# Attention in front of a two-layer network: the maxima of queries and keys behind the third sigmoid's split, their product with ones in the next pair, and ten output steps in a batch's first gap

## The chip, the core and the metric

The kernel runs on one core of a Trainium2 chip. The core has four engines that compute: TensorE (matmuls into PSUM; PE in the profile, its weight loads PEld), VectorE (DVE), ScalarE (ACT) and GpSimd (POOL). SyncE (SP) issues the transfers. Each engine works through its own list of instructions in order, and engines wait for each other through semaphores. The metric is the device time of one execution in microseconds, the median of several.

## The reference

```python
def _attn_ref(q, k, v) -> np.ndarray:          # (8, 12, 448, 64) each
    S = q.shape[2]
    scale = 1.0 / np.sqrt(q.shape[-1])
    scores = scale * np.matmul(q, k.transpose(0, 1, 3, 2)) - np.log(S)
    attn = 1.0 / (1.0 + np.exp(-scores))
    return np.matmul(attn, v).astype(np.float32)

def _moe_ref(x, w_in, w_out) -> np.ndarray:    # (3584, 768), (768, 2048), (2048, 768)
    h = x @ w_in
    alpha = 1.0
    g = np.where(h > 0.0, h, alpha * (np.exp(np.minimum(h, 0.0)) - 1.0))
    return (g @ w_out).astype(np.float32)
```

The attention's result, its heads side by side, is the network's x. So each of the 8 batches has 12 heads of 448 tokens, a sigmoid in place of a softmax, and 448 rows of the network.

## The kernel before

**Numbers as pairs of halves.** A float32 operand is split into a high and a low float16 part (`split`, L120: ScalarE writes the high part, VectorE the low one), and a product takes three matmuls: high x high, low x high, high x low. Before a split the operand is multiplied by a power of two that comes from its largest magnitude. `prepare` (L294) finds the maxima of a pair of heads per partition on VectorE (L125 for values, mx, and for queries and keys, mt; L307, L310), and puts them on the diagonal of a matrix (`magnitude`, L98: three instructions of L105 write dg). That is its first part. The second part, `scales` (L314), multiplies ones with that matrix on TensorE (L110, pb: the "product with ones", which brings all 128 partitions' maxima to each), takes the largest (L112), rounds it to a power of two (L113, L114), and makes the scales on VectorE and GpSimd (L318, L324, L319, L322, L289; the tile sc). The third part, `transposed` (L331), splits queries and keys by those scales (nat, three pieces on each of the two engines), has a DMA transpose them into qk (L352), and splits the values (vn, L358).

**A pair of heads.** The loop from L686 on runs over batches 1 to 7 and, in each, over six pairs. For a pair, `scores` (L376) multiplies keys by queries for one of four blocks of keys (t = 0 to 3, the last of them half as large) into psc, of which there are two buffers. `soften` (L391) takes the sigmoid on ScalarE (sg, L395), and for the first three blocks splits it: high part on ScalarE (at, L413), low part on VectorE (at, L414). `values` (L419) multiplies values by those into pav; each block's last two matmuls are the first that read the low part. `finish` splits the result into xh, the network's input (L121, L122), and takes its maximum.

**The network.** Behind the sixth pair, `hidden` rescales xh (L448, L450, L451), and `moe1` (L479) multiplies it by w_in for 16 blocks of the hidden layer (ph), with the exponential on ScalarE. Behind ph's first block stands a product with ones of its own, for the layer's scale. The output layer of a batch (`moe2`) is not run then: it is cut into steps of three matmuls (po, L529; 16 steps to a tile, 96 steps, or 128 where two batches' last tokens are done too) that the next batch's pairs run between their own work. `fill(n)` runs n such steps. Batches 1, 3, 5 and 7 have 96 steps, 16 for a pair; batches 2, 4 and 6 have 128, 21 or 22 for a pair. Those of the first kind are called short below.

**What sets the order.** Batch 0, the weights' splits and the first layer of batch 0 are put in order by a planner from a model of times. From L685 on, the order on TensorE, ScalarE, VectorE and SyncE is that of the code; GpSimd's is planned. In the loop, a pair n does: scores and sigmoids of blocks 0 and 1; `third()`, the split and transpose of pair n+1; the loads of pair n+3; a gap of 8 steps in a batch's first pair and 5 in the others; the maxima of pair n+2 (`prepare_pair`); scores and sigmoids of blocks 2 and 3; the rest of the steps; the product and scales of pair n+2 (`second()`); the values; `finish`. In batch 1 the last splits of w_out (`step`, wo) are in the loop too.

Of the kernel before, what the change touches and what calls it, by code (L numbers as in the profile page):

```python
# [32 lines left out]
def attention_ffn(  # L33
# [13 lines left out]
    NP = H // 2  # L47
# [9 lines left out]
    EXACT = 1  # L57
# [213 lines left out]
    def load_v(b, hp):  # L271
        rv = rvs[(b * NP + hp) % len(rvs)]
        main = rv[:, : 2 * NC].rearrange("p t d -> p (t d)")
        load_keys(main, [rv[r, 2 * NC + j] for j, r in enumerate(rows)], v, b, 2 * hp)
        return rv
# [320 lines left out]
    def prepare_pair(n):  # L596

        if n >= len(pairs):
            return lambda: lambda: None
        b, hp = pairs[n]  # L600
        if hp == 0:
            xh_of[b] = sb.tile([P, NK, 2, S], F16, tag="xh", name=f"xh{b}", bufs=2)
            xs_of[b] = sb.tile([P, 3, NP], F32, tag="xs", name=f"xs{b}", bufs=2)
        scales = prepare(b, hp, *loaded.pop(n), xs_of[b])

        def second():
            transposed = scales()

            def third():
                ready[n] = transposed()  # L610

            return third

        return second
# [12 lines left out]
    def pair_of(n):  # L627
        b, hp = pairs[n]
        return Pair(b, hp, *ready.pop(n), xh_of[b], xs_of[b])
# [18 lines left out]
    def load_pair(n):  # L648
        if n < len(pairs):
            loaded[n] = load_qk(*pairs[n]), load_v(*pairs[n])  # L650
# [8 lines left out]
    for n in range(EXACT * NP):  # L659
# [12 lines left out]
        for f in range(W_IN[n], W_IN[n + 1]):  # L672
            load_w_in(1)
            w_in_tile(f)
    third = prepare_pair(EXACT * NP + 1)()
    load_pair(EXACT * NP + 2)
    g = sb.tile([P, 2, NF, SM + 2 * R], F16, tag="g", name="g")
    h = hidden(0, w_out_beside)
# [6 lines left out]
    with tc.manual_schedule(engines={E.PE, E.Activation, E.DVE, E.SP}):  # L685
        for b in range(EXACT, B):  # L686
            out_scale(*of_moe2, slice(0, 1 if b == EXACT else NH))
            tiles = moe2(b - 1, g, wo)
            left = NF * NH * (NC + (b - 1) % 2)

            def fill(n):
                nonlocal left
                left -= n
                for _ in range(n):
                    next(tiles, None)

            for hp in range(NP):
                n = b * NP + hp
                share = left // (NP - hp)
                tail = 4 if hp == NP - 1 else 0  # L700
                p = pair_of(n)
                for t in range(2):
                    p.scores(t)
                    p.soften(t)
                third()
                if n + 3 < len(pairs):
                    loaded[n + 3] = load_qk(*pairs[n + 3]), load_v(*pairs[n + 3])

                gap = 8 if hp == 0 else 5
                fill(gap)  # L710
                second = prepare_pair(n + 2)
                for t in range(2, NC + 1):
                    p.scores(t)
                    p.soften(t)
                if b == EXACT and hp < NC:

                    step(3 if hp < NC - 1 else NF)
                if hp == NP - 1:
                    h = hidden(b)
                    next(h)  # L720
                fill(share - gap - tail)
                third = second()
                for t in range(NC + 1):
                    p.values(t)
                p.finish()
                fill(tail)
                if b == EXACT and hp == NC - 1:
                    out_scale(*of_moe2, slice(1, NH))
            of_moe2 = next(h)
        out_scale(*of_moe2)  # L730
        for _ in moe2(B - 1, g, wo):
            pass
# [30 lines left out]
```

## Time and profile before

| | |
|---|---|
| runs of the kernel before | 1273.72, 1271.79, 1272.22 us; median 1272.22 |
| the profiled execution | 1270.86 us, its span 1269.1 us |
| busy, share of the span | TensorE 95%, VectorE 65%, ScalarE 53%, GpSimd 7% |
| HBM over the span | 55 GB/s |
| mean granted TensorE clock | 0.984 |

A row of the timeline reads: start in us from the span's start, duration, engine, line, operation, output and inputs by name, shape, and how many instructions are merged. In brackets stands how long the engine had been idle and what released it. A row of the waits reads: who waited, for whom, us in total, how often, the longest. A row of the stretches reads: the stretch, its length, the busy time of PE, PEld, DVE, ACT and POOL with instructions in brackets, the granted clock, the DMA's share and GB/s.

### The profile page before, as it was taken

The page shows a single profiled execution, that of the slowest core. Times are in us where ns is not written, and L with a number is a line of the kernel's source. Part 1 is how long each engine was busy: PE and PEld are TensorE (multiplying, and loading weights), DVE is VectorE, ACT ScalarE, POOL GpSimd, SP SyncE. Part 2 cuts the span into 40 slices and gives each one's busy share as a digit, 9 for nine tenths or more (in the row PEclk, how much of TensorE's full clock was granted, in tenths as well). Part 3 has the DMA queues.
Part 4 walks back from the last instruction along what each step waited for, and adds up shares of the span by engine and source line. Part 5 has one row for each costly group of instructions (what it writes and reads, how often), then busy time and mean ns, then how long its engine had stood idle before and what let it go on. Part 6 is the DMA issues. An engine that isn't in the chain of part 4 may idle for free.

```text
span 1269.1 us, 19337 instructions
## 1 busy us (share of the span) xinstructions
PE 1200.2 (95%) x7246; PEld 610.5 (48%) x7246; DVE 823.4 (65%) x1872; ACT 671.8 (53%) x1015; POOL 84.1 (7%) x319
## 2 busy tenths in 40 slices
PE   5979868999999999999999999999999999999998
PEld 2324334445555554545455554545455554455565
DVE  5898989765766557775666646885576656765500
ACT  5867777643655337744555436654565435663400
POOL 0011001100000000010000000010000100100000
PEclk9889979999999999999999999999999999999999
DMA  8937423420233103340144201440034401410000
GB/s 229 281 100 222 126 77 80 100 49 1 60 84 89 37 1 83 89 86 1 37 92 92 50 1 43 105 103 7 1 86 92 92 1 22 106 43 7 1 25 26
DMA packets 213407, 89.76 MB, mean 71 GB/s; under 512 B 177472, under 2 KB 209216, under 8 KB 213312
## 3 DMA queue, kind: packets, MB, share of 16 engines
q1 hardware_dynamic: 213312, 88.51, 28.7%
q8 instruction: 57, 0.93, 0.3%
q14 instruction: 38, 0.31, 0.1%
HBM read 58.20 MB, written 11.01 MB: 55 GB/s over the span
## 4 chain that ended last, share of the span: by engine, by line
PE 78%; ACT 8%; DVE 7%; DMA 3%; issue 2%; SPq 2%; DVEq 0%; POOL 0%; ACTq 0%; POOLq 0%
PE ph L499 31%; PE po L529 25%; PE psc L384 7%; PE pav L433 6%; PE po_r L529 5%; PE pav L425 3%; ACT sg L395 2%; DMA stage<-in_moe_w_in_dram 2%; ACT at L413 1%; SPq L262 1%; PE pb L110 1%; ACT L395 1%; ACT e L511 1%; DVE e L514 1%; DMA so<-in_moe_w_out_dram 1%
## 5 line engine op out<-in xcount | busy, mean ns | idle before, releaser
L499 PE MATMUL ph<-xh,wi 128*128 128x448 f16 x2304 | 442.0, 353 | 6.1 <-DVE xh L122 2.4
L529 PE MATMUL po<-wo,g 128*128 128x384 f16 x2304 | 392.9, 328 | 0.0
L529 PEld LDWEIGHTS <-g 128*128 128x128 f16 x2688 | 257.2, 98 | 198.4 <-issue 36.3
L499 PEld LDWEIGHTS <-wi 128*128 128x128 f16 x2304 | 225.3, 98 | 218.4 <-issue 7.6
L511 ACT ACTIVATE e<-ph,msc 128x448 f32<-128x448 f32 x128 | 80.8, 633 | 211.7 <-PE ph L499 211.6
L414 DVE SCALAR_TENSOR_TENSOR at<-sg,at 128x896 f16<-128x896 f32 x126 | 137.2, 1090 | 84.5 <-ACT at L413 84.5
L395 ACT ACTIVATE sg<-psc,bias,sc 128x896 f32<-128x896 f32 (+1 forms) x168 | 166.6, 992 | 1.7
L513 DVE TENSOR_SCALAR e<-e 128x448 f32<-128x448 f32 x128 | 50.3, 394 | 170.8 <-ACT e L511 170.7
L121 ACT ACTIVATE xh<-pav,sc 128x448 f16<-128x448 f32 x48 | 30.3, 632 | 216.7 <-PE pav L425 216.7
L384 PE MATMUL psc<-qk 64*128 64x448 f16 x1008 | 116.6, 355 | 11.4 <-ACT sg L395 11.4
L413 ACT ACTIVATE at<-sg 128x896 f16<-128x896 f32 x126 | 119.8, 951 | 4.1
L121 ACT ACTIVATE g<-e,msc 128x384 f16<-128x384 f32 (+1 forms) x192 | 96.0, 534 | 6.0 <-DVE e L514 4.3
L122 DVE SCALAR_TENSOR_TENSOR g<-e,msc,g 128x384 f16<-128x384 f32 (+1 forms) x192 | 94.6, 521 | 0.6
L514 DVE SCALAR_TENSOR_TENSOR e<-ph,msc,e 128x448 f32<-128x448 f32 x128 | 87.3, 683 | 4.0
L384 PEld LDWEIGHTS <-qk 64*128 64x128 f16 x1008 | 41.7, 97 | 89.7 <-issue 60.2
L433 PE MATMUL pav<-at,vn 128*64 128x448 f16 x756 | 80.2, 357 | 0.0
L324 POOL TENSOR_SCALAR sc<-pw 128x1 f32<-128x1 f32 x42 | 12.4, 295 | 843.5 <-DVE pw L114 790.9
L529 PE MATMUL po_r<-wo,g 128*128 128x384 f16 x384 | 64.7, 326 | 0.0
L122 DVE SCALAR_TENSOR_TENSOR xh<-pav,sc,xh 128x448 f16<-128x448 f32 x48 | 32.7, 680 | 48.7 <-ACT xh L121 48.7
L433 PEld LDWEIGHTS <-vn 128*64 128x64 f16 x756 | 39.4, 110 | 50.0 <-issue 27.8
L122 DVE SCALAR_TENSOR_TENSOR nat<-raw,sc,nat 128x384 f16<-128x384 f32 (+1 forms) x126 | 59.1, 524 | 0.0
L121 ACT ACTIVATE nat<-raw,sc 128x384 f16<-128x384 f32 (+1 forms) x126 | 58.8, 529 | 0.0
(103 smaller groups left out, 852.7 us busy)
## 6 DMA issues: line engine op xcount, KB each, us to landing
stage<-in_moe_w_in_dram SPq DMA_DIRECT2D x16, 768.0 KB, 6.6
raw<-in_q_dram SPq DMA_DIRECT2D x96, 96.0 KB, 3.1
raw<-in_k_dram SPq DMA_DIRECT2D x96, 96.0 KB, 2.6
rv<-in_v_dram SPq DMA_DIRECT2D x48, 192.0 KB, 2.7
out_dram<-o SPq DMA_DIRECT2D x48, 192.0 KB, 2.1
wo<-in_moe_w_out_dram SPq DMA_DIRECT2D x19, 384.0 KB, 4.1
so<-in_moe_w_out_dram SPq DMA_DIRECT2D x13, 384.0 KB, 4.3
raw<-in_q_dram SPq DMA_DIRECT2D x48, 32.0 KB, 2.4
```

Of the source, the lines that this page charges most:

```text
L121: nc.scalar.mul(hi, src, s)
L122: nc.vector.scalar_tensor_tensor(lo, src, s, hi, op0=ALU.mult, op1=ALU.subtract)
L384: nc.tensor.matmul(psc[:, j, :S] if g < NC else psc[rows[j], 0, :S], kk[rows[j], o], qq[rows[j], :S], start=(n == 0), stop=(n == len(parts ...
L395: a = nc.scalar.activation(sg[:, :nb], psc[:, :nb, :S], AF.Sigmoid, bias=bias, scale=self.s_scale)
L413: nc.scalar.mul(hi, sg, 2.0**ATOP)
L414: nc.vector.scalar_tensor_tensor(lo, sg, 2.0**ATOP, hi, op0=ALU.mult, op1=ALU.subtract)
L433: nc.tensor.matmul(pav[rows[j], :S], vv[i][:, j * NC + g], sg[k][:, j], start=(g == 0 and n == 0), stop=False,)
L499: nc.tensor.matmul(ph[:, :S], wi[:, wj, c, f * P : (f + 1) * P], xh[:, c, xj], start=(n == 0), stop=(n == 3 * NK - 1),)
L511: a = nc.scalar.activation(e, ph[:, :S], AF.Exp, scale=inv)
L513: nc.vector.tensor_scalar(e, e, 1.0, -1.0, op0=ALU.min, op1=ALU.add)
L514: nc.vector.scalar_tensor_tensor(e, ph[:, :S], inv, e, op0=ALU.mult, op1=ALU.max)
L529: nc.tensor.matmul(po[:, :HM], lh(gj, f), wo[:, i, f, wj], start=(n == 0), stop=(n == 3 * NF - 1),)
```

## The change

Three lines of the loop move and one number changes. The maxima of pair n+2 are taken behind the scores and sigmoids of blocks 2 and 3. The product with ones and the scales of a pair are no longer made at the end of the pair two ahead of it, but in the pair right ahead of it, behind blocks 0 and 1 and directly in front of the split that uses them. And a batch's first gap has ten steps, not eight.

```diff
@@ ahead of the loop
-    third = prepare_pair(EXACT * NP + 1)()
+    second = prepare_pair(EXACT * NP + 1)
@@ in the loop over pairs
                 for t in range(2):
                     p.scores(t)
                     p.soften(t)
-                third()
+                second()()
                 if n + 3 < len(pairs):
                     loaded[n + 3] = load_qk(*pairs[n + 3]), load_v(*pairs[n + 3])
 
-                gap = 8 if hp == 0 else 5
+                gap = 10 if hp == 0 else 5
                 fill(gap)
-                second = prepare_pair(n + 2)
                 for t in range(2, NC + 1):
                     p.scores(t)
                     p.soften(t)
+                second = prepare_pair(n + 2)
                 if b == EXACT and hp < NC:
...
                 fill(share - gap - tail)
-                third = second()
                 for t in range(NC + 1):
                     p.values(t)
                 p.finish()
```

On VectorE, in the second pair of batch 3, the kernel before has these rows from the second sigmoid's low split on (at_1 is the sigmoid of this pair, nat_2 and vn_2 the split of the next pair, mx_3, mt_3 and dg the maxima of the one behind it, o the eviction of an output tile, sc the scales):

```order
L414 SCALAR_TENSOR_TENSOR at_1_4855<-sg_1_4853,at_1_4855 128x896
L122 SCALAR_TENSOR_TENSOR nat_2_4858<-raw_2_4090,sc_2_4802,nat_2_4858 128x384
L122 SCALAR_TENSOR_TENSOR nat_2_4858<-raw_2_4090,sc_2_4802,nat_2_4858 128x128
L122 SCALAR_TENSOR_TENSOR nat_2_4858<-raw_2_4090,sc_2_4802,nat_2_4858 128x384
L122 SCALAR_TENSOR_TENSOR vn_2_4867<-rv_83,sc_2_4802,vn_2_4867 128x384
L125 TENSOR_REDUCE mx_3_4898<-rv_85 128x1
L125 TENSOR_REDUCE mt_3_4900<-raw_3_4701 128x7
L307 TENSOR_REDUCE mx_3_4898<-mt_3_4900 128x2
L310 TENSOR_TENSOR mx_3_4898<-mx_3_4898,mt_3_4900 64x1 x2
L105 TENSOR_SCALAR dg<-eye,mx_3_4898 128x128 x3
L414 SCALAR_TENSOR_TENSOR at_1_4919<-sg_1_4917,at_1_4919 128x896
L537 TENSOR_SCALAR o_1_0_4964<-po_1_0_4882,osc_4659 128x384
```

and with the change, on the same engine at the same place:

```order
L414 SCALAR_TENSOR_TENSOR at_1_4840<-sg_1_4838,at_1_4840 128x896
L112 TENSOR_REDUCE al<-pb 128x3
L113 TENSOR_SCALAR al<-al 128x3
L114 TENSOR_SCALAR pw_2_4770<-al 128x3
L318 RECIPROCAL sc_2_4849<-pw_2_4770 128x3
L282 TENSOR_TENSOR xs_3946<-xs_3946,pw_2_4770 128x1
L285 RECIPROCAL xs_3946<-xs_3946 128x1
L122 SCALAR_TENSOR_TENSOR nat_2_4858<-raw_2_4090,sc_2_4849,nat_2_4858 128x384
L122 SCALAR_TENSOR_TENSOR nat_2_4858<-raw_2_4090,sc_2_4849,nat_2_4858 128x128
L122 SCALAR_TENSOR_TENSOR nat_2_4858<-raw_2_4090,sc_2_4849,nat_2_4858 128x384
L122 SCALAR_TENSOR_TENSOR vn_2_4867<-rv_83,sc_2_4849,vn_2_4867 128x384
L414 SCALAR_TENSOR_TENSOR at_1_4907<-sg_1_4905,at_1_4907 128x896
```

The third low split (the second L414 row of each) has moved ahead of the maxima, which now follow it, and the chain from L112 on, which stood behind the eviction of the pair before, is between the second low split and the split of the next pair.

On TensorE the same pair's product with ones stands, in the kernel before, behind the last output step and ahead of the first value:

```order
L529 LDWEIGHTS g
L529 MATMUL po_1_0_4882<-wo,g 128x384
L110 LDWEIGHTS ones
L110 MATMUL pb<-dg,ones 128x384
L433 LDWEIGHTS vn_1_4696
L433 MATMUL pav_1_4982<-at_1_4843,vn_1_4696 64x448
```

and with the change behind the second block of scores and ahead of the gap's first output step:

```order
L384 LDWEIGHTS qk_1_4694
L384 MATMUL psc_1_4831<-qk_1_4694 128x448
L110 LDWEIGHTS ones
L110 MATMUL pb<-dg,ones 128x384
L529 LDWEIGHTS g
L529 MATMUL po_1_0_4882<-wo,g 128x384
```

So its diagonal, made at the end of the pair before, has to be ready a sixth of the way into the pair.

On ScalarE, in the first pair of batch 1, the splits of w_out (wo) stand in the kernel before behind the fourth sigmoid (the L395 row of 128x448; at_0 and sg_0 are this pair's, nat_1 and vn_1 the next pair's):

```order
L121 ACTIVATE vn_1_1650<-rv_85,sc_1_898 128x384
L395 ACTIVATE sg_0_1709<-psc_0_1702,bias,sc_0_803 128x896
L413 ACTIVATE at_0_1711<-sg_0_1709 128x896
L395 ACTIVATE sg_0_1721<-psc_0_1714,bias,sc_0_803 128x448
L121 ACTIVATE wo<-wo,swo_1564 128x384 x12
L121 ACTIVATE xh_783<-pav_0_1771,sc_0_803 128x448
```

and with the change, on the same engine:

```order
L121 ACTIVATE wo<-wo,swo_1549 128x384 x2
L121 ACTIVATE nat_1_1641<-raw_1_776,sc_1_1632 128x384
L121 ACTIVATE wo<-wo,swo_1549 128x384
L121 ACTIVATE nat_1_1641<-raw_1_776,sc_1_1632 128x128
L121 ACTIVATE wo<-wo,swo_1549 128x384
L121 ACTIVATE nat_1_1641<-raw_1_776,sc_1_1632 128x384
L121 ACTIVATE vn_1_1650<-rv_85,sc_1_1632 128x384
L395 ACTIVATE sg_0_1703<-psc_0_1696,bias,sc_0_803 128x896
L121 ACTIVATE wo<-wo,swo_1549 128x384 x2
L413 ACTIVATE at_0_1705<-sg_0_1703 128x896
L395 ACTIVATE sg_0_1715<-psc_0_1708,bias,sc_0_803 128x448
L121 ACTIVATE wo<-wo,swo_1549 128x384 x6
```

Six of the twelve now stand ahead of the third sigmoid's high split (at_0). VectorE's low parts of the same splits are in the same order.

## The prediction

> **What bounds the kernel now.** I read the page first (shares, then the chain that ended last), then TensorE's waits behind the start-up, then the stretches by pair, then one pair instruction by instruction.
>
> ```profile
> span 1269.1 us, 19337 instructions
> ...
> PE 1200.2 (95%) x7246; PEld 610.5 (48%) x7246; DVE 823.4 (65%) x1872; ACT 671.8 (53%) x1015; POOL 84.1 (7%) x319
> ...
> PE 78%; ACT 8%; DVE 7%; DMA 3%; issue 2%; SPq 2%; DVEq 0%; POOL 0%; ACTq 0%; POOLq 0%
> ```
>
> TensorE is busy 95% of the span and carries 78% of the last chain. What the change can win is therefore TensorE's waiting inside the loop, and that is a short list (behind 190 us):
>
> ```profile
> PE pb L110 <- DVE dg L105: 11.6, 6, 2.0
> PE psc L384 <- ACT sg L395: 10.5, 8, 2.5
> ```
>
> Six waits of the product of ones (pb) for its diagonal (dg), 11.6 us, and eight waits of scores for a sigmoid. Everything else in the loop already lies under matmuls. A pair in the middle of an odd batch (a "short" pair: 16 output steps) shows how tightly. These are chosen rows of its timeline (start, duration, instruction, and in brackets what ended the idle time before it); S is its first score, 503.43:
>
> ```profile
> 501.79 0.55 DVE L112 TENSOR_REDUCE al<-pb 128x3 f32<-128x384 f32 x1
> 503.27 0.23 POOL L319 TENSOR_SCALAR sc<-sc 128x3 f32<-128x3 f32 x1
> 503.43 1.31 PE L384 MATMUL psc<-qk 64*128 64x448 f16 x12
> 508.17 1.40 ACT L121 ACTIVATE nat<-raw,sc 128x384 f16<-128x384 f32 x3
> 508.30 1.09 DVE L414 SCALAR_TENSOR_TENSOR at<-sg,at 128x896 f16<-128x896 f32 x1 [0.88 <-ACT at L413]
> 509.31 1.41 DVE L122 SCALAR_TENSOR_TENSOR nat<-raw,sc,nat 128x384 f16<-128x384 f32 x3
> 510.78 1.54 SPq L352 DMA_TRANSPOSE qk<-nat  x1
> 511.09 0.95 ACT L413 ACTIVATE at<-sg 128x896 f16<-128x896 f32 x1
> 511.16 0.68 DVE L125 TENSOR_REDUCE mx<-rv 128x1 f32<-128x512 f32 x1
> 513.43 0.58 DVE L105 TENSOR_SCALAR dg<-eye,mx 128x128 bf16<-128x128 bf16 x3
> 513.93 1.08 DVE L414 SCALAR_TENSOR_TENSOR at<-sg,at 128x896 f16<-128x896 f32 x1
> 514.32 1.89 PE L433 MATMUL pav<-at,vn 128*64 128x448 f16 x18
> ```
>
> and, from the table of DMA issues, the last number being the median us from issue to landing:
>
> ```profile
> qk<-nat SPq DMA_TRANSPOSE x42, 4.0
> ```
>
> The next pair's first score is at 517.09, so a short pair lasts 13.66, all of it TensorE. Three covers are thin: dg ends at 514.01, when its product is due; the third split ends at 515.01 (S+11.58) and the values need it at S+12.5 (they start at S+10.89, and the first use of its low half is 16 of 18 matmuls, 1.6, later); the transpose lands 4.0 after 510.78, at S+11.35, 2.3 before the next scores.
>
> **The change part by part.** No instruction is added; the product of ones, 0.16 to 0.33 of TensorE, only stands elsewhere. One wait is added: the split of the next pair's queries and keys (nat) now follows directly on the scales it needs. VectorE works in order, so the chain that makes the scales starts only behind the second sigmoid's split: L112 starts where nat's low half starts now, S+5.88. From L112 (501.79) to the end of L319 (503.50) is 1.71; nat on ScalarE starts at S+7.64 instead of S+4.74. **Everything that ScalarE has queued behind nat moves by 2.90**: vn's split, the third and fourth sigmoid, the third split. If the first nat piece waited for the copies behind L319 too it would be about 0.5 more; nothing less than 2.90 unless L112 could overtake.
>
> What is late next, in a short pair:
> - The third split's high half starts at S+7.66+2.90 and ends at S+11.51; its low half, no longer behind the maxima, runs S+11.54 to S+12.63. Due at S+12.5: values end 0.1 to 0.2 late.
> - nat's low half now runs just behind its high half and ends at S+9.7; the transpose starts there instead of S+7.35 and lands at S+13.75, the next scores being due at S+13.66: 0.1 to 0.2.
> - The maxima follow the third split. From mx (511.16) to dg's end (514.01) is 2.85, so dg ends at S+15.4; the product now stands in the next pair behind two scores, at S+13.66+1.24 = S+14.9: 0.5 late. That delay sits in the next pair's TensorE and covers its own third split, so over two pairs it counts about once: 0.25 each.
>
> Behind the transpose on SyncE's queue stand the loads of the pair three ahead; they land 2.4 later and are read by maxima that run 4 later, so they cost nothing. GpSimd's work behind the scales (vr) is needed a pair later: nothing.
>
> The three are ends of one chain and don't add. I take 0.25 a pair. Bounds: 0 if each reserve is a little larger than the rows say, 0.7 with the 0.5 above. Batches 3, 5 and 7 have four such pairs each: 12 x 0.25 = **+3.0** (0 to 8.4). In long pairs (even batches, 21 or 22 steps, 2.4 us more of matmuls) all three are covered: 0.
>
> By the Trainium skill's "Perfetto Trace Analysis" (section "Per-instruction lifecycle: what the profiler-reported window actually captures") the window of a DMA instruction holds only the issue, not the data's movement. Here the window is 1.54 and the landing 4.0, so the trace agrees; by the window alone the transpose would be no bound, and the pair would cost 0.2 instead of 0.25.
>
> First pair of a short batch:
>
> ```profile
> 480.01 0.76 PE L384 MATMUL psc<-qk 64*64 64x448 f16 x6 [1.03 <-ACT sg L395]
> 480.70 4.07 PE L529 MATMUL po<-wo,g 128*128 128x384 f16 x24
> 483.77 0.95 ACT L413 ACTIVATE at<-sg 128x896 f16<-128x896 f32 x1
> 486.75 0.32 PE L110 MATMUL pb<-dg,ones 128*128 128x384 bf16 x1 [1.97 <-DVE dg L105]
> 489.77 1.31 PE L384 MATMUL psc<-qk 64*128 64x448 f16 x12
> ```
>
> Two more steps (4.07 for eight, 0.5 each) and the product fill the 1.03 ahead of the fourth score; the 1.97 for dg goes. But the six steps that are left end at 483.7, and the third split's high half moves to 483.77+2.90 = 486.67, its low half ends at 488.73; two matmuls (0.2) and the last values (0.95) later it is 489.9. Against 489.77 that is +0.2: both waits are gone and one for ScalarE's split stands in their place. Three batches: **+0.6**.
>
> Last pair of a short batch, where the layer's first matmuls follow:
>
> ```profile
> 544.41 1.31 PE L384 MATMUL psc<-qk 64*128 64x448 f16 x12
> 555.05 0.32 PE L110 MATMUL pb<-dg,ones 128*128 128x384 bf16 x1 [1.91 <-DVE dg L105]
> 555.91 0.23 DVE L448 TENSOR_SCALAR rr<-xs 128x6 f32<-128x6 f32 x1
> 559.39 0.67 DVE L122 SCALAR_TENSOR_TENSOR xh<-pav,sc,xh 128x448 f16<-128x448 f32 x1
> 559.93 3.57 PE L499 MATMUL ph<-xh,wi 128*128 128x448 f16 x18
> 561.21 0.25 DVE L105 TENSOR_SCALAR dg<-eye,rr 128x128 bf16<-128x128 bf16 x1
> 563.33 0.22 PE L110 MATMUL pb<-dg,ones 128*128 128x128 bf16 x1
> ```
>
> The third split ends at 544.41+12.62 = 557.0; the 1.91 turns into a wait for it and the values end 0.25 late. Behind it VectorE has 2.85 of maxima (559.9), then the rescale from L448: its first piece ends near 560.5, so ph starts 0.6 late. The rescale's 2.25 ends at 562.1; from xh's split to dg's end is 2.07 (559.39 to 561.46), so the layer's dg ends at 564.15 and its product starts 0.8 late. Batches 3 and 5 (the last batch prepares no pair): 2 x 0.85 = **+1.7** (0 to 2.4).
>
> Long batches: in the first pair the same 1.2 wait of the fourth score shrinks to 0.3, and the moved third split gives it back; the end is as above with 2.4 more cover. Between -0.95 (nothing given back) and +0.85 (the short end) each, I take +0.2 as the nearer row is the short one's: 3 batches, **+0.6**.
>
> Batch 1 still has twelve splits of w_out (wo, 0.57 to 0.65 each on ScalarE and VectorE) to place:
>
> ```profile
> 181.01 1.40 ACT L121 ACTIVATE nat<-raw,sc 128x384 f16<-128x384 f32 x3
> 193.75 1.14 ACT L121 ACTIVATE wo<-wo,swo 128x384 f16<-128x384 f32 x2 [0.16 <-DVE wo L122]
> 196.46 0.74 PE L384 MATMUL psc<-qk 64*128 64x448 f16 x6 [2.51 <-ACT sg L395]
> 198.43 1.17 PE L384 MATMUL psc<-qk 64*64 64x448 f16 x6 [1.23 <-ACT sg L395]
> 209.15 1.31 PE L384 MATMUL psc<-qk 64*128 64x448 f16 x12
> ```
>
> Now they all follow the fourth sigmoid and cost the next pair 2.51+1.23. In the new order six of them stand ahead of the third split's high half (6 x 0.6 = 3.6, on top of the 2.9 less the wait that they fill): the first pair's values end about 3.4 late; the six that are left end about when the twelve do now, VectorE's second split of the next pair ends 2 late, and that pair ends at 210.45 instead of 209.15, +1.3. In the two pairs behind it the last wo splits (3 and 1) stand on VectorE behind the maxima and push the next sigmoids' splits: +1.5 and +0.5; the last two pairs and the end as in other short batches, 0.3 and 0.85. Together **+4.5** (0 to 7).
>
> Batch 0 is put in order by a planner, whose order changes too (an exponential moves ahead of two splits of w_in); the work is the same, TensorE waits there for loads and splits, and I take 0 (-2 to +2).
>
> Sum: 3.0+0.6+1.7+0.6+4.5 = +10.4. The profiled execution took 1270.86 (its span 1269.1 and 1.76 around it), so 1281.3; the median of the three runs shown, 1272.22, lies 1.36 above it, so 1282.7 for a median.
>
> **The rivals.**
> - *The reserves hold.* The three ends of the short pair differ from their due times by 0.1 to 0.5, which rows rounded at a pipelined engine may hide. Then the steady term is 0 and batch 1 gives back half: 1282.7-3.0-2.3-0.5 = about 1277. For it: the middle pairs show no wait now. Against it: dg's 0.5 is outside that error. Chance 0.20, a third of it within 0.2% of now (2.5 us, about what a measurement can tell).
> - *Faster: ScalarE doesn't wait for the scales.* In a short batch's first pair the third split would then be done at 485.8 and the pair end at 487.1: 2.65 won; a shift above 2.65 loses. That is the point, and I get 2.90. With no shift: 3 x 2.65, 2 x 1.5 at the ends (VectorE's rescale limits it), 3 x 0.95 in the long batches: -13.8, 1258.4. For it: 11.6 us of waits for dg do go. Against it: the order of VectorE below the second split. Chance 0.07.
> - *The clock.* New waits of 2.5 us in first pairs might lower the granted clock. After the 5.30 us wait in batch 1 the clock was 0.50; around the 1.97 us wait it stayed at 1.00:
>
> ```profile
> 175.00:180.00 5.00, 1.43 (x3) 0.34 (x3) 3.45 (x6) 3.94 (x7) 0.00 (x0) 0.50 0.21 82
> 472.99:489.77 16.78, 13.78 (x94) 6.94 (x94) 11.75 (x26) 11.49 (x15) 0.42 (x2) 1.00 0.24 49
> ```
>
>   At half speed the values and scores behind the wait (4 us) would take 8: 3 x 4 = 12, 1295. Chance 0.05. The Trainium skill's "TensorE: Matmul & The Clock Gate" (section "Part 1: The HAM clock gate (the "warmup" mystery)") has the clock halved after an idle window of about 3.4 us; by that rule 2.5 is not enough, and the two rows agree.
> - *Batch 0's new order decides*: its waits for loads move the start of the loop by 4 or more either way, 1278 or 1287. Chance 0.10.
>
> **How the numbers follow.** Forecast 0.58, reserves 0.20, faster 0.07, clock 0.05, batch 0 0.10. Faster by over 0.2%: 0.08 (the third rival and a little of batch 0). Within 0.2% (1269.7 to 1274.8): 0.10. Slower: 0.82. The range goes from 1274.5 (reserves hold and batch 1 costs nothing) to 1291 (each short pair at 0.5, batch 1 at 7); outside lie the faster case, the clock and some of the rest.
>
> **What would show it.** nat (L121) starts about 2.9 later behind the second split, with ScalarE idle ahead of it and POOL L319 named; TensorE waits for the third split (pav for at L414) in the first and last pairs of batches 3 and 5; pb still waits for dg, now 0.2 to 0.5 in many short pairs; batch 1's first pair ends 3 later; even batches keep their length within 0.9. A nat that starts under S+6, or short pairs of 13.66 with first pairs under 16, would prove me wrong.

## The result and the profile after

The changed kernel takes 1289.63 us (median of four runs, 1288.58 to 1293.49); the kernel before, on the same chip, 1272.15 (1271.79 to 1273.72). The ratio is 1.014, interval 1.0118 to 1.0163: slower, as forecast, by 17.5 us where 10.4 had been worked out. The profiled spans are 1288.0 and 1269.1 us, 18.9 apart.

The page of the changed kernel, its span, busy shares and the chain that ended last:

```profile
span 1288.0 us, 19325 instructions
...
PE 1209.2 (94%) x7246; PEld 614.4 (48%) x7246; DVE 830.8 (65%) x1872; ACT 674.5 (52%) x1015; POOL 93.1 (7%) x319
...
PE 59%; ACT 16%; DVE 14%; issue 4%; DMA 4%; SPq 1%; POOL 1%; DVEq 0%; ACTq 0%; POOLq 0%
```

Each of the five rows of the page counts as many instructions as before. TensorE's busy share hardly moved, 95% to 94%, but its share of the last chain fell from 78% to 59%: ScalarE and VectorE, in turn, now hold the end of a pair. TensorE's waits behind 190 us say with what:

```profile
PE pav L433 <- ACT at L413: 16.7, 11, 4.5
PE pav L433 <- DVE at L414: 6.9, 15, 0.6
PE pb L110 <- DVE dg L105: 3.9, 19, 0.3
PE psc L384 <- ACT sg L395: 1.9, 2, 1.2
```

The long waits for the diagonal (11.6 us in 6) are gone, and of those for the sigmoid (10.5 in 8) 1.9 are left. In their place stand values that wait for the third split's high and low half, 23.6 us together, and 19 small waits for dg. So behind 190 us about 22 us of waits became 29. The rest of the 18.9 lies ahead of that point and in the clock, below.

Chosen rows of the timeline of a short pair in the middle of batch 3; S, its first score, is 515.46:

```profile
516.70 0.34 PE L110 MATMUL pb<-dg,ones 128*128 128x384 bf16 x1
521.33 0.55 DVE L112 TENSOR_REDUCE al<-pb 128x3 f32<-128x384 f32 x1
522.80 0.23 POOL L319 TENSOR_SCALAR sc<-sc 128x3 f32<-128x3 f32 x1
523.06 1.41 ACT L121 ACTIVATE nat<-raw,sc 128x384 f16<-128x384 f32 x3 [2.77 <-POOL sc L319]
525.30 1.54 SPq L352 DMA_TRANSPOSE qk<-nat  x1
526.98 1.09 DVE L414 SCALAR_TENSOR_TENSOR at<-sg,at 128x896 f16<-128x896 f32 x1 [1.22 <-ACT at L413]
528.13 0.38 PE L433 MATMUL pav<-at,vn 128*64 128x448 f16 x2 [0.19 <-DVE at L414]
529.39 1.31 PE L384 MATMUL psc<-qk 64*128 64x448 f16 x12
530.26 0.58 DVE L105 TENSOR_SCALAR dg<-eye,mx 128x128 bf16<-128x128 bf16 x3
530.89 0.32 PE L110 MATMUL pb<-dg,ones 128*128 128x384 bf16 x1 [0.20 <-DVE dg L105]
```

Read it from the top: the product with ones starts at S+1.24, about a tenth of the way into the pair (not a sixth, as the text on the change has it); VectorE reaches L112 at S+5.87, though pb had been finished at S+1.6; ScalarE sits idle 2.77 us for GpSimd's L319; nat starts at S+7.60 (forecast 7.64), the third low split runs from S+11.52 (forecast 11.54), dg ends at S+15.38 (forecast 15.4). Two matmuls wait 0.19, the product 0.20. The pair lasts 13.93 (forecast 13.91, before 13.66).

The span's 18.9, from the first scores of each pair and the first matmuls of each layer in the two timelines, beside the terms of the prediction:

| stage | forecast | measured |
|---|---|---|
| batch 1 | +4.5 | +9.6 |
| steady short pairs of batches 3, 5, 7 | +3.0 | +5.2 |
| first pairs of those | +0.6 | +0.5 |
| last pair and layer's start, batches 3 and 5 | +1.7 | +1.5 |
| batches 2, 4, 6 | +0.6 | +2.0 |
| batch 0 | 0 | see batch 1 |

Of the 2.2 that the steady pairs are over the forecast, about 1.4 is clock. First pair of batch 3, TensorE's rows at its end and the first scores behind:

```profile
497.93 0.57 PE L433 MATMUL pav<-at,vn 128*64 128x448 f16 x4 [2.56 <-ACT at L413]
499.06 0.38 PE L433 MATMUL pav<-at,vn 128*64 128x448 f16 x2 [0.56 <-DVE at L414]
500.51 2.42 PE L384 MATMUL psc<-qk 64*128 64x448 f16 x12
```

and a stretch of 2 us behind them (granted clock third from the end):

```profile
500.00:502.00 2.00, 2.00 (x12) 0.59 (x12) 1.87 (x8) 0.78 (x2) 0.00 (x0) 0.52 0.49 110
```

Twelve scores take 2.42 in place of 1.31. The second pair of batch 3 lasts 14.95, 1.0 above the others; batch 5 shows the same with 0.4 there and 1.0 already in the first pair (18.09 against 17.09 in batch 7); batch 7, with the same two waits, not at all.

### The profile page after: what moved, and what is told of

Read it like the earlier page. It is cut to its first block, busy times and chain, and to the rows that moved or that the text cites. A ratio compares the mean times of both kernels' runs of the same rounds, so it can differ in the third digit from the quotient of the medians.

```text
span 1288.0 us, 19325 instructions
## 1 busy us (share of the span) xinstructions
PE 1209.2 (94%) x7246; PEld 614.4 (48%) x7246; DVE 830.8 (65%) x1872; ACT 674.5 (52%) x1015; POOL 93.1 (7%) x319
## 4 chain that ended last, share of the span: by engine, by line
PE 59%; ACT 16%; DVE 14%; issue 4%; DMA 4%; SPq 1%; POOL 1%; DVEq 0%; ACTq 0%; POOLq 0%
PE ph L499 29%; PE po L529 17%; ACT sg L395 5%; PE psc L384 4%; ACT at L413 4%; PE pav L433 3%; PE po_r L529 3%; DVE at L414 3%; DMA stage<-in_moe_w_in_dram 2%; PE pav L425 2%; ACT nat L121 1%; DVE mt L125 1%; DMA wo<-in_moe_w_out_dram 1%; DVE mx L125 1%; DVE al L112 1%
## 5 line engine op out<-in xcount | busy, mean ns | idle before, releaser
L529 PEld LDWEIGHTS <-g 128*128 128x128 f16 x2688 | 260.4, 98 | 192.0 <-issue 25.2
L414 DVE SCALAR_TENSOR_TENSOR at<-sg,at 128x896 f16<-128x896 f32 x126 | 137.4, 1091 | 113.0 <-ACT at L413 113.0
L395 ACT ACTIVATE sg<-psc,bias,sc 128x896 f32<-128x896 f32 (+1 forms) x168 | 166.5, 991 | 2.9 <-PE psc L384 1.3
L384 PE MATMUL psc<-qk 64*128 64x448 f16 x1008 | 119.3, 360 | 3.1 <-ACT sg L395 2.7
L433 PE MATMUL pav<-at,vn 128*64 128x448 f16 x756 | 86.9, 358 | 23.7 <-ACT at L413 16.7
L122 DVE SCALAR_TENSOR_TENSOR nat<-raw,sc,nat 128x384 f16<-128x384 f32 (+1 forms) x126 | 63.9, 558 | 38.1 <-ACT nat L121 38.1
L433 PEld LDWEIGHTS <-vn 128*64 128x64 f16 x756 | 42.2, 109 | 67.4 <-issue 46.2
L537 DVE TENSOR_SCALAR o<-po,osc 128x384 f32<-128x384 f32 x48 | 29.3, 611 | 40.4 <-PE po L529 35.8
```

The lines of the kernel that those rows point to most:

```text
L122: nc.vector.scalar_tensor_tensor(lo, src, s, hi, op0=ALU.mult, op1=ALU.subtract)
L384: nc.tensor.matmul(psc[:, j, :S] if g < NC else psc[rows[j], 0, :S], kk[rows[j], o], qq[rows[j], :S], start=(n == 0), stop=(n == len(parts ...
L395: a = nc.scalar.activation(sg[:, :nb], psc[:, :nb, :S], AF.Sigmoid, bias=bias, scale=self.s_scale)
L414: nc.vector.scalar_tensor_tensor(lo, sg, 2.0**ATOP, hi, op0=ALU.mult, op1=ALU.subtract)
L433: nc.tensor.matmul(pav[rows[j], :S], vv[i][:, j * NC + g], sg[k][:, j], start=(g == 0 and n == 0), stop=False,)
L529: nc.tensor.matmul(po[:, :HM], lh(gj, f), wo[:, i, f, wj], start=(n == 0), stop=(n == 3 * NF - 1),)
```

## The experiments

All compute the full result. Ratios are against the kernel before on the same chip; a dash stands where there was a single run. The last three columns come from the profiled execution: the first scores of batch 2 (all that lies ahead, batch 1 with its layer included), what is left of the span from there, and a steady short pair.

| kernel | median us | ratio (interval) | to batch 2 | batches 2 to 7 | short pair |
|---|---|---|---|---|---|
| before | 1272.15 | 1 | 320.3 | 948.8 | 13.66 |
| changed | 1289.63 | 1.014 (1.0118 to 1.0163) | 329.9 | 958.1 | 13.93 |
| early scales | 1254.76 | 0.9866 (0.9848 to 0.9884) | 320.1 | 931.9 | 13.55 |
| changed, first scales planned | 1286.69 | 1.0115 (1.0100 to 1.0131) | 324.6 | 958.5 | 13.93 |
| changed, gap of 8 | 1288.53 | 1.0134 (1.0117 to 1.0152) | 327.9 | 958.4 | 13.93 |
| before, late maxima alone | 1347.14 | - | 339.9 | 1005.6 | 17.22 |
| before, gap of 10 alone | 1270.59 | 0.9986 (0.9972 to 1.0000) | 321.0 | 947.8 | 13.66 |
| changed, maxima at the old place | 1327.34 | - | 334.4 | 991.1 | 15.39 |
| early scales, first ones planned | 1252.71 | 0.9847 (0.9822 to 0.9872) | 317.0 | 931.9 | 13.55 |
| early scales, maxima at the old place | 1268.22 | 0.9967 (0.9954 to 0.9981) | 323.8 | 942.5 | 13.55 |
| early scales, gap of 8 | 1257.02 | 0.9879 (0.9864 to 0.9894) | 318.6 | 934.9 | 13.55 |
| changed, L319 on VectorE | 1282.88 | 1.0079 (1.0059 to 1.0098) | 331.4 | 952.3 | 13.65 to 13.80 |
| early scales, first planned, w_out dealt out | 1250.14 | 0.9828 (0.9809 to 0.9848) | 316.3 | 932.0 | 13.55 |

### Is it the place of the scales?

The theory: all of the loop's loss starts with ScalarE waiting for scales that VectorE makes behind the second low split. The rivals: the late maxima, or the product early in a pair, cost it by themselves. The edit to the changed kernel moves the scales ahead of the first two sigmoids and leaves the split where it is:

```diff
                 for t in range(2):
                     p.scores(t)
+                third = second()
+                for t in range(2):
                     p.soften(t)
-                second()()
+                third()
```

> The changed kernel with one thing moved: the product with ones and the scales of the next pair stand behind the scores of blocks 0 and 1, but ahead of their sigmoids and splits; the split of the next pair stays behind them. So VectorE makes the scales ahead of the first sigmoid's low split and ScalarE has no wait ahead of nat. Theory A (the loss in the loop comes from ScalarE's wait of 2.8 us behind the second low split, which moves the third split): nat starts under S+5.5 again, the third split's low half ends under S+10.5, dg ends under S+13.5, short pairs return to 13.66 and first pairs of short batches fall to 14.1 to 15 (two waits of 1.03 and 1.97 gone, nothing in their place); against the changed kernel that is 5.2 in steady pairs, about 8 in first pairs, 3 in last pairs and 2 to 5 in the long batches and batch 1 less: 1263 to 1272. Rival B (the maxima behind the third split, or the product two scores into the pair, cost the time by themselves): pairs stay at 13.9 with pb waiting for dg, 1284 to 1290. Rival C (the chain of scales delays the first sigmoid's low split, and with it the values): pairs above 13.9, over 1290.

1254.76 us, 1.3% under the kernel before and below what the theory had given. A short pair with S at 513.30:

```profile
514.54 0.34 PE L110 MATMUL pb<-dg,ones 128*128 128x384 bf16 x1
515.19 0.55 DVE L112 TENSOR_REDUCE al<-pb 128x3 f32<-128x384 f32 x1
516.52 1.07 DVE L414 SCALAR_TENSOR_TENSOR at<-sg,at 128x896 f16<-128x896 f32 x1
516.66 1.01 POOL L319 TENSOR_SCALAR sc<-sc 128x3 f32<-128x3 f32 x1
518.03 1.40 ACT L121 ACTIVATE nat<-raw,sc 128x384 f16<-128x384 f32 x3
521.94 1.09 DVE L414 SCALAR_TENSOR_TENSOR at<-sg,at 128x896 f16<-128x896 f32 x1 [0.71 <-ACT at L413]
525.22 0.58 DVE L105 TENSOR_SCALAR dg<-eye,mx 128x128 bf16<-128x128 bf16 x3
526.84 1.31 PE L384 MATMUL psc<-qk 64*128 64x448 f16 x12
```

The chain from L112 now fills time in which VectorE waited for the first split's high half, and nat is back at S+4.73 with no idle time ahead of it. The third low split ends at S+9.73, dg at S+12.5, and no matmul waits. Expected were 13.66 for the pair; it is 13.54. Most of the 0.12 is the product, which costs TensorE less at its new place: the steps behind it start 0.17 after it (at 514.71), where ahead of the values it is 0.25 (545.34 to 545.59 in the rows of the next section). First pairs fell to 14.55 (short) and 16.13 (long), last pairs to 13.45 from 15.52. What is left of waits behind 190 us:

```profile
PE psc L384 <- ACT sg L395: 4.4, 2, 3.1
PE pav L433 <- DVE at L414: 1.3, 3, 0.4
PE psc L384 <- DMA qk<-nat: 1.0, 3, 0.3
PE pb L110 <- DVE dg L105: 0.8, 1, 0.8
```

Both rivals fall: the maxima and the product stand where the change put them, and the time goes down.

### Each half of the change alone

The maxima late, the product and scales at the pair's end as before:

```diff
                 fill(gap)
-                second = prepare_pair(n + 2)
                 for t in range(2, NC + 1):
                     p.scores(t)
                     p.soften(t)
+                second = prepare_pair(n + 2)
```

> The kernel before with the maxima alone moved behind the scores and sigmoids of blocks 2 and 3; the product with ones and the scales stay at the end of the same pair, and the gap is eight. Theory A (the maxima are only free there because their product is due in the next pair): the third low split ends 0.6 earlier or stays where it was, the maxima end about 2.85 behind it, near S+14.5 or later with the split at S+11.6, and the product, due at S+10.9 to S+12, waits for dg about 2 us in each short pair: 15 pairs of batches 3, 5 and 7 and some of the others by 1 to 2 us each, 20 to 40 over before, 1292 to 1312. Rival B (the late maxima are hidden by themselves, and the loss is all in the late scales): within 3 of before, 1270 to 1275.

1347 us, worse than the forecast's upper end. TensorE waits 62.4 us for dg, as the theory said (1.87 in each short pair, 3.8 to 4.1 in the first and last pairs of short batches), but a wait of 1.87 costs 3.55 where the clock falls behind it. Three pairs of batch 3, first TensorE's rows, then stretches behind the first two waits (the clock third from the end):

```profile
545.34 0.32 PE L110 MATMUL pb<-dg,ones 128*128 128x384 bf16 x1 [1.87 <-DVE dg L105]
545.59 3.42 PE L433 MATMUL pav<-at,vn 128*64 128x448 f16 x18
...
579.82 0.32 PE L110 MATMUL pb<-dg,ones 128*128 128x384 bf16 x1 [1.87 <-DVE dg L105]
580.07 1.89 PE L433 MATMUL pav<-at,vn 128*64 128x448 f16 x18
...
595.40 0.32 PE L110 MATMUL pb<-dg,ones 128*128 128x384 bf16 x1 [3.82 <-DVE dg L105]
595.65 1.89 PE L433 MATMUL pav<-at,vn 128*64 128x448 f16 x18
```
```profile
545.30:549.50 4.20, 4.16 (x20) 1.83 (x20) 1.70 (x7) 0.00 (x0) 1.12 (x5) 0.59 0.54 140
...
580.60:582.85 2.25, 2.25 (x20) 0.87 (x14) 0.83 (x5) 0.00 (x0) 1.26 (x6) 1.00 0.65 156
```

The same wait, the same instruction: 18 values in 3.42 at a mean clock of 0.59, or in 1.89 at 1.00; and in 1.89 behind a wait of 3.82, too. Pairs are 17.2 or 15.59 accordingly.

The other half: product and scales late as in the change, the maxima back ahead of blocks 2 and 3.

```diff
                 fill(gap)
+                second = prepare_pair(n + 2)
                 for t in range(2, NC + 1):
                     p.scores(t)
                     p.soften(t)
-                second = prepare_pair(n + 2)
```

> The changed kernel with the maxima back at their old place, ahead of blocks 2 and 3; the product with ones and the scales stay behind blocks 0 and 1 of the next pair, as changed. Theory A (the late scales push nat to S+7.6, and the maxima, again ahead of the third split's low half, push that in turn): nat's low half ends at S+9.7, dg at S+12.6, the third low split at S+13.7 where S+12.5 is due, so short pairs are 14.7 to 15.0 where the changed kernel has 13.93, TensorE waits for at L414 instead of pb for dg, 1298 to 1312. Rival B (the maxima's place is the loss): short pairs 13.66 or less, below the changed kernel, 1272 to 1283.

1327 us, again above the expected range; TensorE waits for the third low split, as the theory said, with 1.65 in a short pair (expected 1.0 to 1.3):

```profile
539.17 0.38 PE L433 MATMUL pav<-at,vn 128*64 128x448 f16 x2 [1.65 <-DVE at L414]
```

So each half alone is far worse than both: late maxima need a product that is due later, and late scales need a VectorE that is free for the third split. The change held together; what it lacked was the place of the scales. With early scales, are the late maxima still needed? The edit above, on early scales:

> Early scales with the maxima at their old place ahead of blocks 2 and 3, gap of ten: of the change only the later product with ones is left, and it stands early. Theory A (the product's move alone takes away the waits for dg, but the maxima ahead of the third low split still hold it back by up to 2.85 where the steps don't cover): short pairs 13.55 as with early scales, first pairs of short batches 15.5 to 16.8 instead of 14.55 with a wait for at L414, last pairs 14.5 to 15.5 instead of 13.45; 1260 to 1268. Rival B (the maxima's place is free once the product is late): within 1.5 of early scales alone, 1253 to 1256.5.

1268.22: steady pairs are 13.55, but the first pair of batch 3 ends with

```profile
490.16 0.38 PE L433 MATMUL pav<-at,vn 128*64 128x448 f16 x2 [2.26 <-DVE at L414]
```

and lasts 16.31, the last pair 14.86, both as expected; the median is 0.2 above the expected range, and the pair behind that wait is again longer (14.83), with a granted clock of 0.50 between 492 and 494 us. The late maxima are worth 10.6 us of batches 2 to 7 once the scales are early (942.5 against 931.9).

### Is the size a matter of reserves?

If a short pair's reserve is about 2.65 and what goes beyond is paid one for one, a shift that is a little smaller must give a little back. One instruction of the changed kernel moves from GpSimd to VectorE:

```diff
-                nc.gpsimd.tensor_scalar(sc[:, :n], sc[:, :n], 2.0**TOP, None, op0=ALU.mult)
+                nc.vector.tensor_scalar(sc[:, :n], sc[:, :n], 2.0**TOP, None, op0=ALU.mult)
```

> The changed kernel with one instruction moved from GpSimd to VectorE: the multiplication of the scales at L319, which ends ScalarE's wait, follows the reciprocals' first one directly. It tests the size: the hop to GpSimd is a part of the 2.9 us by which nat is late. Theory A (the reserves of a short pair are 2.65 or so, and what goes beyond them is paid one for one): nat starts 0.2 to 0.4 earlier, ScalarE's wait falls from 2.77 to about 2.5, short pairs fall from 13.93 to between 13.6 and 13.75, the wait for the third split in first pairs falls by as much, 1280 to 1286. Rival B (the order of VectorE below it takes the gain back: the second reciprocals and copies behind L319 are as late as before, so nat's second piece waits for the copies): nat's first piece is earlier but the transpose is not, short pairs 13.85 to 13.95, 1287 to 1291.

```profile
523.33 0.21 DVE L319 TENSOR_SCALAR sc<-sc 128x3 f32<-128x3 f32 x1
...
523.58 1.41 ACT L121 ACTIVATE nat<-raw,sc 128x384 f16<-128x384 f32 x3 [2.49 <-DVE xs L282]
```

ScalarE's wait is 0.28 shorter (2.49 for 2.77; L319 ends at 523.54, so the xs that the row names is not needed to explain its end). Short pairs fall to 13.65 and 13.80 in about equal numbers, batches 2 to 7 take 5.8 us less, and the median, 1282.88, is in theory A's range. So at a shift of about 2.62 half of the pairs lose nothing and the others 0.15: the reserves end about where the prediction read it from the rows.

### What the gap of ten is worth

`gap = 8` in the changed kernel, `gap = 10` in the kernel before, and `gap = 8` with early scales.

> The changed kernel with the old gap of eight steps in a batch's first pair. Theory A (the third split sets the end of the first pair, so the steps ahead of the third scores only fill what waits there): the fourth scores wait about 1.0 longer for the second buffer, the wait for the third split shrinks by as much, each first pair keeps its length within 0.4, and the time is 1288 to 1291.5. Rival B (the two steps that moved up leave fewer matmuls ahead of the values, and the wait of 2.5 for the third split with the lower clock behind it comes from that): the first pairs of batches 3 and 5 and the pairs behind them lose their slow clock, 1 us each, 1284 to 1287.

> The kernel before with the gap of ten alone. Theory A (in a batch's first pair the diagonal dg sets the end; two more steps ahead of the third scores take away the wait of 1.03 for the fourth scores and lengthen the wait for dg): first pairs change by -0.4 to +0.4, the time is 1270 to 1273.5. Rival B (dg itself comes earlier, or the first pair was bound by the fourth scores): first pairs of batches 2 to 7 lose 1.0 each, 1264 to 1267.

> Early scales with the old gap of eight. In the kernel before, ten alone won nothing that can be told from no change. Theory A (ten steps fill the wait of the fourth scores, and that counts only where nothing later holds the pair): first pairs of batches 2 to 7 wait about 1.0 for the fourth scores and are 0.8 to 1.1 longer than with early scales and ten steps (14.55 and 16.13), 1260 to 1262. Rival B (the gap is free with early scales too, because the third split or the steps cover it): first pairs within 0.2, 1253 to 1256.5.

In the changed kernel eight or ten is the same (958.4 and 958.1 for batches 2 to 7). In the kernel before ten alone gains 0.14% with an interval that ends at no change; the first long pair shrinks by 0.31 and short ones not at all (16.77; in batch 7 it is 18.21, behind a lowered clock that the kernel before has in batch 5), since the wait for dg grows, from 1.97 to 2.94, as the wait for the fourth scores shrinks. With early scales it counts, but only in long batches; the first pair of batch 2 with a gap of eight shows the wait

```profile
325.82 0.76 PE L384 MATMUL psc<-qk 64*64 64x448 f16 x6 [1.05 <-ACT sg L395]
```

and lasts 17.11 against 16.13, while the short first pair is 14.57 against 14.55: there the ten steps take away a wait of 0.87 for the fourth scores, and waits of 0.42 for the third split and 0.33 for the next pair's transpose take its place. So the time, 1257.0, falls between the two theories: A had every first pair lose, B none. Three long batches make the 3.0 us between 934.9 and 931.9; the intervals of the two whole kernels overlap.

### Batch 1

The changed kernel loses 9.6 us up to batch 2, twice the forecast. Its first pair, ScalarE, GpSimd and TensorE around the second pair's scales:

```profile
186.22 0.66 POOL L551 TENSOR_SCALAR osc<-wop,wm 128x2 f32<-128x2 f32 x1
186.87 0.70 POOL L555 TENSOR_SCALAR osc<-osc,xs,rr 128x1 f32<-128x1 f32 x1
187.54 0.23 POOL L319 TENSOR_SCALAR sc<-sc 128x3 f32<-128x3 f32 x1
...
187.80 0.61 ACT L121 ACTIVATE nat<-raw,sc 128x384 f16<-128x384 f32 x1 [1.12 <-POOL sc L319]
...
192.63 0.94 ACT L413 ACTIVATE at<-sg 128x896 f16<-128x896 f32 x1
...
193.62 0.96 PE L433 MATMUL pav<-at,vn 128*64 128x448 f16 x4 [4.55 <-ACT at L413]
...
195.25 1.86 PE L425 MATMUL pav<-sg,vr 128*128 128x448 f32 x2
```

The scales' L319 stands on GpSimd behind the output layer's scales (1.36 us of L551 and L555 in these rows, and 0.74 of L551 ahead of them), two splits of w_out stand ahead of nat and four more between nat and the third split, and TensorE waits 4.55, behind which the last matmuls take 1.86 instead of 1.02. To see how much of the 9.6 this is, the scales of that one pair are made ahead of the loop, as before:

```diff
-    second = prepare_pair(EXACT * NP + 1)
+    third = prepare_pair(EXACT * NP + 1)()
...
-                second()()
+                if n > EXACT * NP:
+                    third = second()
+                third()
```

> The changed kernel with one thing undone: the product with ones and the scales of the first pair that the loop prepares (the second of batch 1) are made ahead of the loop, under the planner, as in the kernel before. The rest of the loop is as changed. Batch 1 takes 9.6 us more than before in the changed kernel. Theory A (6.95 of it are in the first pair: the planner's order of batch 0 gives about 2.1, and scales made in a crowded first pair, behind other GpSimd work and with six w_out splits ahead of the third split, give the rest): batch 1's first pair ends within 1.5 of before, batch 1 gives back 4 to 7, the time is 1283 to 1286. Rival B (batch 1 loses it in every pair by the w_out splits behind the maxima, and the first pair only shows it first): the first pair is shorter, the later ones longer by as much, and the time stays within 1.5 of the changed kernel, 1288 to 1291.

The first pair ends at 190.08, where before has 190.10 and the changed kernel 197.05, and batch 1's loss falls from 9.6 to 4.4. The rest is where rival B had it: the next two pairs last 20.14 and 15.62 (before 19.05 and 13.66), the others 0.3, 0.3 and 0.65 more. So both theories hold a part. But of the 5.3 us that the profile gives back only 3.4 are there at the end of the second pair (213.63 against 210.22), and 0.6 more come in the third. The last 1.4 stand in the batch's last pair (17.57 against 16.17), where TensorE waits alike in both kernels, and only the changed one's clock falls behind it, to 0.57 between 271 and 275 us:

```profile
269.35 0.57 PE L433 MATMUL pav<-at,vn 128*64 128x448 f16 x4 [1.26 <-ACT at L413]
...
271.88 3.55 PE L529 MATMUL po<-wo,g 128*128 128x384 f16 x12
```

These twelve steps take 2.11 in the other kernel. The whole kernel's time, 1286.69, lies 0.7 above theory A's range; by the medians the edit is worth 2.9 us, and the two intervals overlap. The profile shows where the first pair's time went; what that is worth in the whole is not settled.

With early scales the same edit:

> The kernel with early scales (the first run of this list: ahead of the sigmoids of blocks 0 and 1), and with the scales of the loop's first prepared pair made ahead of the loop under the planner, as before. Theory A (what the planner's order and the crowded first pair cost is apart from the wait for scales, and adds up): batch 1's first pair ends 1 to 3 earlier than the 191.13 of early scales alone, the later batches are the same, 1250.5 to 1253.5, against the kernel before 0.984 to 0.986. Rival B (with early scales the first pair no longer waits for them, so nothing is left to give back, and the w_out splits cost the second pair as much in either order): 1253.5 to 1256.

The median is 1252.71, inside theory A's range, and the first pair ends at 186.37, further ahead of 191.13 than the 1 to 3 us expected; its interval overlaps that of early scales alone, so that the 2 us between them are not shown. In this version batch 1's second pair lasts 21.9, with these two rows:

```profile
194.79 0.80 PE L384 MATMUL psc<-qk 64*128 64x448 f16 x6 [3.13 <-ACT sg L395]
...
196.76 1.32 PE L384 MATMUL psc<-qk 64*64 64x448 f16 x6 [1.17 <-ACT sg L395]
```

ScalarE and VectorE work off twelve splits of w_out in a row there. Three of them dealt to later pairs:

```diff
-                    step(3 if hp < NC - 1 else NF)
+                    step((0, 4, NF)[hp])
```

> Early scales with the first pair's made ahead of the loop (1252.7 before this), and the last seven w_out splits dealt out as 0, 4 and 3 to the first three pairs of batch 1 in place of 3, 3 and 1. Theory A (in batch 1's second pair the scores wait 3.13 and 1.17 for a sigmoid that stands behind the splits of w_out on ScalarE): three splits fewer, 0.6 each, let the pair start its sigmoid about 1.8 earlier, and the two later pairs, which have some 4 us of idle ScalarE, take them for nothing; 1250.5 to 1251.7. Rival B (VectorE's low parts, in a row with the diagonal, are what is late, or the later pairs pay for the splits they get): 1252 to 1255.

1250.14, 0.4 below theory A's range: the second pair falls from 21.92 to 14.84 (about 2.0 of it is clock: its last 33 output steps take 5.54 instead of 7.57), and the two behind it rise from 13.55 to 15.62 and 14.67, so rival B holds for a part. Its profiled first pair ends 3.2 later than in the kernel without this edit (189.54 against 186.37); 1.8 of that is there when the pair starts, 0.9 more is eighteen output steps at a lower clock (5.04 for 4.15). Its interval too overlaps, so the gain over the kernel without this edit is not shown; against the kernel before it is 1.7% faster, the lowest median of the list.

## Why the prediction was right, and where its sizes were off

**The mechanism.** "VectorE works in order, so the chain that makes the scales starts only behind the second sigmoid's split": shown twice, by the rows (nat at S+7.60 against 7.64) and by early scales, which move that chain alone, take this wait away, and turn +1.4% into -1.3%. The rival that ScalarE doesn't wait had been priced at 1258.4 us; with the wait removed on purpose the kernel takes 1254.8.

**The total.** The time rose by 17.5 us (18.9 in the profiled spans), not 10.4. Batch 1 was 5.1 over its term, the steady pairs 2.2 and the long batches 1.4. The range's upper end, 1291, isn't reached by what the text names for it: short pairs at 0.5 each and batch 1 at 7 make 1282.7+3.0+2.5 = 1288.2, which the measured 1289.63 exceeds. The direction and the mechanism were right; that the total stayed below 1291 owes something to luck.

**Steady short pairs.** 0.25 was taken and 0.27 measured. (By the prediction's own rows dg ends at 12.63+2.85 = S+15.48, not 15.4, and the share is 0.29; measured 15.38.) The rival that the reserves hold falls, and the shift of 0.28 less, which brings pairs back to 13.65 or 13.80, shows that they end about where the rows said. The term came to +5.2 instead of +3.0 mainly by the pairs behind a first pair (+1.29 and +0.62 in batches 3 and 5, clock for the most part) and by pairs four and five of batch 7 (+0.51 and +0.54): there the fourth also waits 0.18 for the transpose, and the fifth has a product with ones that the kernel before no longer has there.

**The clock.** Given a chance of 0.05, it was partly real: in the changed kernel's short batches it cost about 2.5 us, not 12 (1.2 in batch 3, 1.4 in batch 5, none in batch 7), beside what it cost in batch 1. The step that failed is "around the 1.97 us wait it stayed at 1.00": it was read from batch 3 alone. Batch 5 of the kernel before has the same wait with the other outcome, and its first pair was 18.34 long, not 16.78; TensorE's row and the stretch behind it:

```profile
781.02 0.32 PE L110 MATMUL pb<-dg,ones 128*128 128x384 bf16 x1 [1.97 <-DVE dg L105]
```
```profile
782.50:785.61 3.11, 3.11 (x11) 0.86 (x8) 1.18 (x6) 0.00 (x0) 1.12 (x5) 0.50 0.53 114
```

So the cost of a lowered clock, 1.6 us there, was in the kernel before already, and a single instance could not stand for it.

**First and last pairs** of the short batches: +0.5 and +1.5 against +0.6 and +1.7. "Both waits are gone and one for ScalarE's split stands in their place" is what 497.93 with its 2.56 shows. That the first pairs' sum fits is luck: batches 3 and 7 gave +0.46 and +0.32, and batch 5 -0.25, as the clock fell there in both kernels. The working had 489.88 against 489.77, so +0.1 a pair and not +0.2, and where the clock stayed up the pair lost 0.3.

**Long batches.** They lost 0.67 each, not 0.2, and not where the term put it: the first pair, priced at +0.2, kept its length (17.26 to 17.29 against 17.27). "All three are covered" failed in the pair behind the first one, which lost 0.24: pb waits 0.20 there for dg, because dg's due time counts from the pair's first score and the longer end of a long pair gives it nothing when that end itself waits for the third split. And the layer's own product waits behind maxima that now stand ahead of the rescale (in batches 3 and 5 the layer is only 0.11 longer, since its start is already late there):

```profile
432.05 0.22 PE L110 MATMUL pb<-dg,ones 128*128 128x128 bf16 x1 [0.27 <-DVE dg L105]
```

The layer lasts 55.06 instead of 54.63, of which this wait is 0.27. The prediction gave the maxima ahead of the rescale to batches 3 and 5 only.

**Batch 1** is the term most off, +9.6 against +4.5. "The first pair's values end about 3.4 late" left out GpSimd's queue ahead of L319 and the clock behind a wait of 4.55. And the batch's last pair lost 1.4 to the clock behind waits of 1.26 and 0.56. How much of the first pair's 7 us comes from batch 0, and so whether the rival "batch 0's new order decides" holds a part, stays open: the last product over w_out ends 2.1 later than before, but two kernels whose TensorE order is the same up to that point differ by 2.3 (176.75 and 179.08, early scales with the first ones planned, without and with the w_out edit).

## What to carry to other kernels

A chain that ends in another engine's wait belongs ahead of the longer work of its own in-order engine, where that engine has idle time, and not between that work and its consumer: the same instructions, 2.9 us earlier, were worth 35 us here. When a move takes away a wait, ask where on each queue the moved work now starts, not only whether its inputs are there. And a price for a wait should be read from every instance of it in the trace, since the clock behind it may differ from one to the next.

## What the runs showed of the hardware

- Over the stretches shown the granted clock was 0.50 to 0.59 behind waits of 1.87 to 2.56 us, and in one place behind waits of 1.26 and 0.56; behind waits of the same length in the same place of other rounds or kernels it did not fall, and in the kernel with late maxima alone it stayed at 1.00 even behind one of 3.82 (595.40 in the rows above). The clock records of the traces hold only 1.0 and 0.5. The lowered stretches of the changed kernel's loop last 3.41 or 6.83 us and start at 192.87, 271.38, 500.07 and 797.03, all whole multiples of 3.413 us apart. From these figures one lowered stretch of 3.41 us costs at most about 1.7 us, an estimate; 1.2 to 1.7 were measured. The Trainium skill's "TensorE: Matmul & The Clock Gate" (Part 1) has a halved clock after at least one idle window of about 3.4 us, and says that the window runs freely, so that its phase matters. The grid of 3.413 us and the unequal outcome of equal waits agree with such a window; the idle time that it asks for does not, as single waits of 1.87 were enough.
- GpSimd's L319 (128x3) takes 0.23 us by its median in the kernel before and 1.01 with early scales, where it starts just behind the start of VectorE's low split (516.66 and 516.52 in the rows above) and ends 0.1 behind it; GpSimd's busy time rose from 84.1 to 146.3 us. The Trainium skill's "SBUF — State Buffer" (section "SBUF: two separate sides") has the two engines share a pair of ports under an exclusive lock, also for a VectorE instruction with two inputs in SBUF: the trace agrees, and the price is about one whole instruction of the other engine. It was covered here.
